# Attention and a feed-forward gate on one core: new load costs for the planner, a new list of moves, and tile 13 instead of tile 8 normalised by GpSimd

## The chip, the cores and the metric

The kernel runs on one core of a Trainium2 chip. The metric is the time of one execution on the device in microseconds (us). Before the change it is 640.19 us, the median of three runs (639.76, 640.19 and 640.46).

A core has five engines that run on their own and wait for one another through semaphores: TensorE (PE in the profile; its weight loads are PEld), VectorE (DVE), ScalarE (ACT), GpSimd (POOL) and SyncE (SP), which here only issues transfers. Each engine works through its own queue in order.

## The reference

All tensors are bfloat16. The input x has 2048 rows of 512. The kernel computes

```python
xn = _layernorm(x, axis=-1)
s = _A_ref(xn, A_wq, A_wk, A_wv, A_wo)
g = _silu(_B_ref(xn, B_w1, B_w2))
return x + s * g
```

`_A_ref` is attention with 32 heads of 16 elements each. All heads share one K and one V, made from xn by `wk` and `wv` (512x16). The scores are multiplied by 16 ** -0.5, go through a softmax over all 2048 keys, and are multiplied by V; the heads are joined and multiplied by `wo` (512x512). `_B_ref` is a feed-forward block: `silu(xn @ w1) @ w2` with a width of 1792.

## The kernel before

**Tiles and groups.** The rows of x are 16 tiles of 128; four tiles are a chunk of 512 rows. A group of attention is one chunk of queries with four heads; there are 32 groups, and each runs over 16 tiles of keys. A tile of scores has four blocks, one for each head, of 128 keys x 512 queries. The four heads stand in four row strips of TensorE, so blocks of different heads are multiplied at the same time.

**Two ways through the exponential.** Two blocks of a tile are a "run": TensorE writes them to one of two large PSUM banks (psA), ScalarE takes the exponential of both in one instruction (`exp_A`, L674) into pa_sb, and the bank is free again. In the other way (`exp_D`, L714) VectorE takes one block from a small PSUM bank (psD, psF, psO) and writes a 16-bit integer which, read as a bfloat16, is near the exponential; GpSimd then makes two shifted copies of the whole tile (`shift`, L739, an integer add), and the three copies, each with its own weight, are summed in the product with V. A tile on ScalarE needs one product with V for its four blocks, a tile on VectorE three. Such a product of four blocks is a "quad" (`emit_quad`, L769); all quads of a group add up in psO. When the group is complete, VectorE takes it out of psO, and normalises it (`gn1` to `gn4`, L882 to L908, with the product of numerators and reciprocals at L872).

**Dense work.** The projections q and w and the feed-forward products h and z are "jobs" of 4 or 14 column steps (L404). Each step takes as long as a quad, and both are called slots below. ScalarE makes a tanh for each h and z (L1116), VectorE takes every job out of its bank.

**The order is made when the kernel is built.** `Sched` holds a clock for each engine. `op` appends an instruction to its engine's queue, works out from what it reads and writes which semaphores it must wait for, and advances the clocks by a planned duration: the argument `cost` (for a transfer, `cost` is the time to its landing). The instructions are the same whatever `cost` is; only choices that look at the clocks depend on it.

The kernel is put together in four parts:

1. Fixed code: loads of x (`load_x`, L359) and of the weights (L368 to L374), statistics and normalisation of tiles 0 to 3 (`stats`, `aggr`, `normalise`, L464), the first transposes, K and Q, up to the first scores.
2. "Front", the loop at the end of the function: until the planner's clock of ScalarE passes `HANDOVER` (L297, 30.0) and all tiles are normalised (`settled`, L1351), each step is chosen by the clocks. The choices are tuned by the numbers of `RULES`; `PLAN` (L263) gives the letter of the rule for each stretch of 2 us (`STRETCH`) of that clock.
3. From there `follow` (L1448) takes the moves from a written list, `ORDER` (L298), letter by letter, without looking at the clocks.
4. `finish` (L1378) takes the end from `TAIL` (L299).

The letters of `ORDER`: R scores one run for ScalarE (two blocks), e takes its exponential, o opens a tile for VectorE, f scores one of its blocks into a bank, x lets VectorE take the oldest scored block, v is one quad, J opens a job, d and a digit do so many of its slots, t is a tanh, E lets VectorE take a finished job, 1 to 4 are the steps of a group's normalisation, H is a run of the last group, whose first four tiles of keys are cut by queries into three parts. In `TAIL`, q is a quad of such a part, n a step of its normalisation, P a piece of the last output projection, and r, C, M, G, A, X, Y, Z finish the last four tiles and store them.

**Normalising a tile of x.** For the tiles in `GPN` (L252) GpSimd does it, for the others VectorE. The set of tiles whose statistics are turned into reciprocal deviations together is a chunk, or for chunks 1 and 3 half a chunk (`SPLIT`). GpSimd takes the power and then, right behind it on its queue, normalises those of the set's tiles that are in `GPN`:

```python
            for t in ts:
                if t in GPN:
                    normalise(t, "gp")
```

Two normalised tiles are then transposed by TensorE (L476), copied by VectorE (L484), and give half a chunk of K (L507, copied at L519) and, with the other half, V (L533, L540). The copies of K for the odd groups go through four transfers per chunk (`move_K`, L525).

Of the kernel before, what the change touches and what calls it, by code (L numbers as in the profile page):

```python
# [5 lines left out]
ACT = mybir.ActivationFunctionType  # L6
# [7 lines left out]
P = 128  # L14
# [21 lines left out]
class Sched:  # L36
# [107 lines left out]
    def op(self, eng, fn, reads=(), writes=(), lane=None, cost=None):  # L144
        who = lane or eng
        if lane:
            self.lanes[lane] = eng
        n = self.done.get(who, 0)
        self.done[who] = n + 1
        deps = self.deps(eng, reads, writes)  # L150
        self.at[(who, n)] = self.model(eng, lane, cost, max([self.at[d] for d in deps.items()], default=0.0))
        clk = self.clock.setdefault(eng, {})
        waits = []
        cand = [(f, m) for f, m in deps.items() if clk.get(f, -1) < m]
        for f, m in cand:
            implied = False
            for f2, m2 in cand:
                if (f2, m2) != (f, m) and self.snap[(f2, m2)].get(f, -1) >= m:
                    implied = True
            if not implied:  # L160
                waits.append((f, m))
        for f, m in cand:
            for g, k in self.snap[(f, m)].items():
                if clk.get(g, -1) < k:
                    clk[g] = k
            if clk.get(f, -1) < m:
                clk[f] = m
        for f, m in waits:
            self.flagged.setdefault(f, set()).add(m)
        self.snap[(who, n)] = dict(clk)  # L170
        self.queues.setdefault(eng, []).append((fn, waits, who, n))
        for r in reads:
            self.readers.setdefault(r, {})[who] = n
        for w in writes:
            self.last_w[w] = (who, n)
            self.readers[w] = {}
        return who, n
# [36 lines left out]
def bass_recurrent_scan__grouped_kv_mqa__dense_activation_silu__prompt_kernel(  # L214
# [37 lines left out]
    GPN = (5, 8, 10)  # L252
# [10 lines left out]
    PLAN = "AAAAOAHAZHHYWcJEEEbbb"  # L263
# [16 lines left out]
        P=(0.25, 3.0, 0.65, 10, 1.2, 2.0, 0, 12, 0.2, 3, 3, 0.0, 0.35, 0.43, 0, 0.33, 0, 1),  # L280
# [10 lines left out]
        a=(0.3, 3.0, 0.65, 10, 1.2, 2.0, -4, 24, 0.2, 3, 3, 0.04, 9, 0.43, 0, 0.33, 0, 0),  # L291
        b=(0.2, 3.25, 0.65, 10, 1.2, 2.0, 0, 12, 0.2, 4, 3, 0.04, 9, 0.43, 0, 0.33, 0, 1),
# [6 lines left out]
    TAIL = "HvvvvHvvHvvq0Hq0q0q0q1q1q1q1n0PPn1n0PPn1q2q2n0q2n1n0Pq2n2n1Pr0r1C1n2G0PPPn2r2A0PPM1n2PG2r3X1Y1Z1G3A2A3"  # L299
    ALPHA = "".join(chr(x) for x in range(35, 127) if x != 92) + "".join(chr(x) for x in range(192, 255))  # L300

    with ExitStack() as es:
        def sb(name, shape, dt=BF16):
# [6 lines left out]
        wq_sb = sb("wq_sb", [P, NDC, D])  # L310
        wkn_sb = sb("wkn_sb", [P, NDC, DH])
# [37 lines left out]
        op = K.op  # L349
# [5 lines left out]
           reads=["ident"], writes=["ident"])  # L355
        xv = xf.rearrange("(t p) d -> p t d", p=P)
        ov = of.rearrange("(t p) d -> p t d", p=P)

        def load_x(a, b, queue="sp"):  # L359
            op(queue, lambda e: e.dma_start(x_sb[:, a:b, :], xv[:, a:b, :]), writes=[("x", t) for t in range(a, b)],  # L360
               lane=f"lx{a}", cost=(2.6 if queue == "sp" else 2.0) if b - a == 1 else {4: 4.6, 8: 5.0, 12: 5.6}[a])

        load_x(0, 1)
        load_x(1, 2, "a")
        load_x(2, 3)
        load_x(3, 4, "a")
        load_x(4, 8)
        op("sp", lambda e: e.dma_start(wkn_sb[:], A_wk.rearrange("(dc p) e -> p dc e", p=P)), writes=["wkn"], lane="lwk", cost=2.5)  # L368
        wqv = A_wq.rearrange("(dc p) n -> p dc n", p=P)
        op("sp", lambda e: e.dma_start(wq_sb[:, :, 0:P], wqv[:, :, 0:P]), writes=["wq0"], lane="lwq0", cost=4.0)  # L370
        op("sp", lambda e: e.dma_start(wv_sb[:], A_wv.rearrange("(dc p) e -> p dc e", p=P)), writes=["wv"], lane="lwv", cost=5.0)
        load_x(8, 12)
        load_x(12, 16)
        op("sp", lambda e: e.dma_start(wq_sb[:, :, P:D], wqv[:, :, P:D]), writes=["wq"], lane="lwq", cost=6.0)  # L374
        for j in range(NPH + 1):
            w = 1.0 if j == 0 else PH_W[j - 1]
            op("gp", lambda e, j=j, w=w: e.memset(vaug_sb[:, j, :, :].rearrange("p t (h e) -> p t h e", e=DH)[:, :, 0:3:2, :], w), writes=["vones"])
            op("gp", lambda e, j=j, w=w: e.memset(phw_sb[:, j:j + 1], w), writes=["phw"])
        op("gp", lambda e: e.memset(scr_i[:], 0), writes=["scri"])
        op("v", lambda e: e.memset(zero_sb[:], 0.0), writes=["zero"])  # L380
# [7 lines left out]
           reads=["wkn", "wkp"], writes=["wkp"])  # L388
# [55 lines left out]
        def rstd_pow(ts):  # L444
# [69 lines left out]
        def evac_K(c, bank, key, a, b, writes, eng="v"):  # L514
            dst, src, wr = kT_sb[0][:, c * NQ + a:c * NQ + b], bank[:, a:b], [("kT", 0, w) for w in writes]
            if eng == "a":
                op("a", lambda e: e.activation(dst, src, ACT.Copy), reads=[key], writes=wr)
            else:
                op("v", lambda e: e.tensor_copy(dst, src), reads=[key], writes=wr, cost=0.155 + (b - a) / 960)  # L519
# [52 lines left out]
        for t in tiles(0):  # L572
            normalise(t, "gp" if t in GPN else "v")
        first_T(0, psD[:, 0:NQ], "D", EV[0])
# [49 lines left out]
        gdone = [0.0] * (NGRP + 1)  # L624
        tok = {("q", 0, 0), ("kT", 0, 0), ("kT", 0, 1), ("kT", 1, 0)} | {(k, t) for k in ("nm", "T") for t in range(4)} | {("ag", t) for t in tiles(1)} | {("nm", t) for t in tiles(1) if t in GPN}
        hold = dict.fromkeys(BANKS + ("O",))
# [201 lines left out]
        def ln_ag(tk):  # L828
# [119 lines left out]
        for c in range(NC - 1):  # L948
            b = (c + 1) / NC
# [206 lines left out]
        dst = dict(open=[], idx=-1, fifo=[])  # L1156
# [352 lines left out]
        while not followed:  # L1509
            (SLIP, ROUND, KEEP, HOLD, AGES["gn1"], AGE, F_BEHIND, ENDQ, PVWAIT, LEAD, AHEAD, MARGIN, XGAIN, AIM, TWIN,  # L1510
             TGATE, FRESH, JOINT) = \
                RULES[PLAN[min(int(K.act_end / STRETCH), len(PLAN) - 1)]]
            if not followed and settled():
                if not w2_asked:
                    load_w2()
                    w2_asked = True
                follow(ORDER)
                followed = True
# [28 lines left out]
            if slots > 0:  # L1547
# [3 lines left out]
                if jb and slots >= 2:  # L1551
                    b = free_banks(t + 0.04)
# [68 lines left out]
```

## Time and profile before

| what | value |
|---|---|
| median of three runs | 640.19 us |
| lowest, highest run | 639.76, 640.46 us |
| profiled execution, its own time | 639.66 us |
| its span, first to last instruction | 637.8 us |
| TensorE busy | 631.1 us, 99% |
| ScalarE busy | 625.9 us, 98% |
| VectorE busy | 607.9 us, 95% |
| GpSimd busy | 434.8 us, 68% |
| granted TensorE clock | 0.999 |

The rows of groups read: line of the kernel, engine, operation, tile written and tiles read, shapes, count; behind the bar the busy time, the mean duration in ns, and the idle time of the engine just before these instructions with what ended it. A row of a timeline reads: start, length, engine, line, operation, tiles, shapes, count of the instructions merged, and in brackets the idle time before and what ended it. A row of the chain of waits reads start, length, what. A row of waits reads: who waited for whom, us in total, times, the longest. Instructions of one engine overlap a little, so lengths aren't pitches. The ends of matmuls are modelled, so a busy TensorE isn't one at its peak.

### The profile page before, as it was taken

Reading aid. Unit: us, or ns where it says so; the run is one execution under the profiler, and the core shown is the slowest. Engines: PE = TensorE matmul, PEld = TensorE weight load, DVE = VectorE, ACT = ScalarE, POOL = GpSimd, SP = SyncE. Lnnn points to the kernel's source line nnn. Section 1 sums busy time; section 2 is a strip of 40 time slices with the busy share of each in tenths; the row PEclk is TensorE's granted clock in tenths of the full one; section 3 lists DMA queues with packets and bytes.
Section 4 is the critical chain, followed back from the end, with each engine's and each line's share of the span. In section 5 each row is a group of like instructions: output and inputs, shape, how many; then the busy total and the mean of one; then the engine's idle time right before and its main releaser. Section 6 shows DMA issues by size and latency. Waiting matters only on the chain.

```text
span 637.8 us, 18784 instructions
## 1 busy us (share of the span) xinstructions
PE 631.1 (99%) x8225; PEld 197.1 (31%) x8227; DVE 607.9 (95%) x1049; ACT 625.9 (98%) x721; POOL 434.8 (68%) x438
## 2 busy tenths in 40 slices
PE   8999999999999999999999999999999999999997
PEld 3433332323233232332233323222323333233233
DVE  7989999999999999999999999999999999999994
ACT  8999999999999999999999999999999999999995
POOL 6556575667767777766766766688676676877662
PEclk9999999999999999999999999999999999999999
DMA  6380000000000000000000000001000000000003
GB/s 181 119 283 2 2 2 2 2 1 3 3 1 2 10 9 11 10 2 2 1 3 2 1 3 2 2 10 18 10 2 2 2 2 1 2 2 2 3 9 60
DMA packets 10082, 12.50 MB, mean 20 GB/s; under 512 B 2288, under 2 KB 9456, under 8 KB 9968
## 3 DMA queue, kind: packets, MB, share of 16 engines
q1 hardware_dynamic: 7840, 9.34, 4.5%
q0 software_dynamic: 1728, 1.57, 2.2%
q8 instruction: 64, 1.05, 0.7%
q10 hardware_dynamic: 432, 0.39, 0.2%
q14 instruction: 18, 0.15, 0.1%
HBM read 8.95 MB, written 4.19 MB: 21 GB/s over the span
## 4 chain that ended last, share of the span: by engine, by line
PE 94%; DVE 4%; ACT 1%; DMA 0%; issue 0%; DVEq 0%
PE psO L769 36%; PE psA L643 30%; PE psF L404 23%; PE psD L643 3%; DVE ph_sb L714 1%; DVE stats_sb L424 1%; DMA x_sb<-in_A_x_dram 0%; PE psA L692 0%; DVE xn_sb L465 0%; ACT xnT_sb L497 0%; DVE onb_sb L872 0%; PE psD L507 0%; PE psF L643 0%; ACT L459 0%; DVE xnT_sb L484 0%
## 5 line engine op out<-in xcount | busy, mean ns | idle before, releaser
L674 ACT ACTIVATE pa_sb<-psA 128x1024 bf16<-128x1024 f32 x630 | 593.2, 1067 | 3.1 <-PE psA L643 1.0
L739 POOL INT64_ADD ph_sb<-ph_sb x304 | 316.0, 1057 | 136.6 <-DVE ph_sb L714 136.2
L714 DVE TENSOR_SCALAR ph_sb<-psD 128x512 int16<-128x512 f32 x526 | 339.1, 679 | 13.0 <-PE psD L643 10.1
L769 PE MATMUL psO<-ph_sb,vaug_sb 128*32 128x512 bf16 x1824 | 224.3, 383 | 0.0
L769 PE MATMUL psO<-pa_sb,vaug_sb 128*32 128x512 bf16 (+1 forms) x1292 | 205.7, 378 | 0.0
L643 PE MATMUL psA<-qT_sb,kTa_sb 32*128 32x512 bf16 x640 | 123.9, 384 | 0.0
L739 POOL INT64_ADD x_sb<-x_sb x90 | 93.1, 1050 | 38.1 <-DVE x_sb L714 37.6
L643 PE MATMUL psA<-qT_sb,kTb_sb 32*128 32x512 bf16 x604 | 116.5, 384 | 0.0
L643 PE MATMUL psD<-qT_sb,kTa_sb 32*128 32x512 bf16 x336 | 110.1, 385 | 0.5 <-DVE ph_sb L714 0.5
L643 PE MATMUL psD<-qT_sb,kTb_sb 32*128 32x512 bf16 x347 | 110.6, 384 | 0.0
L714 DVE TENSOR_SCALAR x_sb<-psD 128x512 int16<-128x512 f32 x157 | 103.4, 680 | 3.8 <-PE psD L643 3.0
L769 PE MATMUL psO<-x_sb,vaug_sb 128*32 128x512 bf16 x540 | 93.2, 383 | 0.0
L769 PEld LDWEIGHTS psO<-ph_sb,vaug_sb 128*32 128x32 bf16 x1824 | 55.5, 95 | 53.0 <-issue 31.3
L643 PEld LDWEIGHTS psA<-qT_sb,kTa_sb 32*128 32x128 bf16 x640 | 30.1, 91 | 122.2 <-ACT pa_sb L674 95.8
L404 PE MATMUL psF<-w_sb,u_sb 128*32 128x512 bf16 x896 | 66.5, 384 | 0.0
L404 PE MATMUL psF<-xnT_sb,w_sb 128*32 128x512 bf16 x896 | 66.3, 384 | 0.0
L643 PEld LDWEIGHTS psA<-qT_sb,kTb_sb 32*128 32x128 bf16 x604 | 28.3, 91 | 119.0 <-ACT pa_sb L674 94.2
L769 PEld LDWEIGHTS psO<-pa_sb,vaug_sb 128*32 128x32 bf16 x1292 | 50.7, 95 | 37.2 <-issue 27.2
L714 DVE TENSOR_SCALAR ph_sb<-psF 128x512 int16<-128x512 f32 x70 | 47.5, 678 | 0.0
L1116 ACT ACTIVATE t_sb<-psF 128x512 bf16<-128x512 f32 x72 | 46.1, 640 | 0.0
L1135 DVE SCALAR_TENSOR_TENSOR u_sb<-t_sb,psF 128x512 bf16<-128x512 bf16 x56 | 37.8, 675 | 0.0
L643 PEld LDWEIGHTS psD<-qT_sb,kTb_sb 32*128 32x128 bf16 x347 | 29.0, 90 | 2.4 <-DVE ph_sb L714 0.2
(123 smaller groups left out, 387.6 us busy)
## 6 DMA issues: line engine op xcount, KB each, us to landing
w_sb<-in_B_w_dram SPq DMA_DIRECT2D x2, 1792.0 KB, 11.1
x_sb<-in_A_x_dram SPq DMA_DIRECT2D x3, 512.0 KB, 5.4
out_dram<-ob_sb POOLq DMA_DIRECT2D x12, 128.0 KB, 3.1
wop_sb<-in_A_wo_dram SPq DMA_DIRECT2D x1, 512.0 KB, 4.2
wq_sb<-in_A_wq_dram SPq DMA_DIRECT2D x1, 384.0 KB, 5.3
out_dram<-ob_sb SPq DMA_DIRECT2D x3, 128.0 KB, 1.7
x_sb<-in_A_x_dram SPq DMA_DIRECT2D x2, 128.0 KB, 2.8
x_sb<-in_A_x_dram ACTq DMA_DIRECT2D x2, 128.0 KB, 3.0
```

The source lines that it names most:

```text
L404: r = e.matmul(bank[32 * i:32 * i + 32, :], lhsT=w, rhs=rhs, start=start, stop=stop, tile_position=(0, 32 * i), skip_group_check=True)
L424: op("v", lambda e: e.bn_stats(stats_sb[:, t, :], x_sb[:, t, :]), reads=[("x", t)], writes=[("st", t)], cost=0.687)
L643: return e.matmul(ap, lhsT=kT_sb[g % 2][32 * i:32 * i + 32, kt * P:(kt + 1) * P], rhs=qT_sb[32 * i:32 * i + 32, c % 2, g // 2, :], start=T ...
L674: d = op("a", lambda e: e.activation(pa_sb[:, sl, :], psA[k][:, :], ACT.Exp, scale=ESCALE), reads=["A%d" % k], writes=[("pa", sl)], cost=2 ...
L714: d = op("v", lambda e: e.tensor_scalar(ph_ap(0, sl, 512 * pos, 512 * pos + m), src, float(PH_ONE + PH_BIAS), 0.0, op0=ALU.add, op1=ALU.ma ...
L739: d = op("gp", lambda e, j=j: e.int64_add(ph_ap(j, sl, 0, 4 * NQ).bitcast(I64), ph_ap(0, sl, 0, 4 * NQ).bitcast(I64), PH_SHIFT[j] * 0x0001 ...
L769: r = e.matmul(psO[32 * i:32 * i + 32, cs], lhsT=vaug_sb[:, p["v"], p["kt"], DH * (gi % 2):DH * (gi % 2) + 32], rhs=p["ap"], start=s0, sto ...
L1116: d = op("a", lambda e: e.activation(t_sb[:, n % 2, :], bank_ap(b), ACT.Tanh, scale=0.5 if jb[0] == "h" else 0.25), reads=[b], writes=[("t ...
L1135: op("v", lambda e: e.scalar_tensor_tensor(out=dst, in0=t_sb[:, n % 2, :], scalar=1.0, in1=src, op0=ALU.add, op1=ALU.mult), reads=tk["read ...
```

## The change

Four kinds of edits:

- `GPN` is (5, 10, 13) instead of (5, 8, 10): GpSimd normalises tile 13, VectorE tile 8.
- The planned costs of the loads: x tiles 4 to 7, 8 to 11 and 12 to 15 get 4.3, 5.5 and 6.0 instead of 4.6, 5.0 and 5.6; `wk` 4.9 instead of 2.5; the first part of `wq` 5.2 instead of 4.0. The copy of the first 128 columns of K on ScalarE gets the cost of its width. No instruction is added by these.
- `PLAN` has other letters for the stretches from 8 to 10 us (V for O) and from 28 us on (bbS for JEE).
- `ORDER` and `TAIL` are written anew. Both hold the same number of letters of nearly every kind (601 R, 605 e, 887 v, 784 x, 195 o, 99 J with 556 slots, 72 t, 4 H; f 782 before and 783 after), in another order.

```diff
-    GPN = (5, 8, 10)
+    GPN = (5, 10, 13)
...
-    PLAN = "AAAAOAHAZHHYWcJEEEbbb"
+    PLAN = "AAAAVAHAZHHYWcbbSEbbb"
...
-    ORDER = "xvxR1f01o02f14evxvR0exJ#2d1R1f05ed3xR0f13f02eE#vxR1eJ$2d2x
...
-xR0f02f13eR1exJÆ2d4xHeEÆvvHevvvHeJÇ2d4HeEÇ"
-    TAIL = "HvvvvHvvHvvq0Hq0q0q0q1q1q1q1n0PPn1n0PPn1q2q2n0q2n1n0Pq2n2n1Pr0r1C1n2G0PPPn2r2A0PPM1n2PG2r3X1Y1Z1G3A2A3"
+    ORDER = "xvR0eJ#2d1R1f11f00ed3xxR0o02f16evE#vR1f01exJ$2d2xR0f13ed2xvE
...
+xJÇ2d2xR0f13ed13vxR1f01ed1xvvHeEÇvvHevvHevvHe"
+    TAIL = "vvHvvHvvHvvHq0q0q0q0q1q1q1q1n0PPn1Pn0n1q2q2q2q2n0Pn1n0Pn1Pn2r0r1C1n2G0PPPn2r2A0Pn2PM1PG2r3X1Y1Z1G3A2A3"
...
         def load_x(a, b, queue="sp"):
-               lane=f"lx{a}", cost=(2.6 if queue == "sp" else 2.0) if b - a == 1 else {4: 4.6, 8: 5.0, 12: 5.6}[a])
+               lane=f"lx{a}", cost=(2.6 if queue == "sp" else 2.0) if b - a == 1 else {4: 4.3, 8: 5.5, 12: 6.0}[a])
...
-writes=["wkn"], lane="lwk", cost=2.5)
+writes=["wkn"], lane="lwk", cost=4.9)
...
-writes=["wq0"], lane="lwq0", cost=4.0)
+writes=["wq0"], lane="lwq0", cost=5.2)
...
         def evac_K(c, bank, key, a, b, writes, eng="v"):
             if eng == "a":
-                op("a", lambda e: e.activation(dst, src, ACT.Copy), reads=[key], writes=wr)
+                op("a", lambda e: e.activation(dst, src, ACT.Copy), reads=[key], writes=wr, cost=b - a)
```

More of the change, by code (lines that the diff above doesn't have):

```diff
@@ L367, in bass_recurrent_scan__grouped_kv_mqa__dense_activation_silu__prompt_kernel @@
         load_x(4, 8)
-        op("sp", lambda e: e.dma_start(wkn_sb[:], A_wk.rearrange("(dc p) e -> p dc e", p=P)), writes=["wkn"], lane="lwk", cost=2.5)
+        op("sp", lambda e: e.dma_start(wkn_sb[:], A_wk.rearrange("(dc p) e -> p dc e", p=P)), writes=["wkn"], lane="lwk", cost=4.9)
         wqv = A_wq.rearrange("(dc p) n -> p dc n", p=P)
-        op("sp", lambda e: e.dma_start(wq_sb[:, :, 0:P], wqv[:, :, 0:P]), writes=["wq0"], lane="lwq0", cost=4.0)
+        op("sp", lambda e: e.dma_start(wq_sb[:, :, 0:P], wqv[:, :, 0:P]), writes=["wq0"], lane="lwq0", cost=5.2)
         op("sp", lambda e: e.dma_start(wv_sb[:], A_wv.rearrange("(dc p) e -> p dc e", p=P)), writes=["wv"], lane="lwv", cost=5.0)
```

2 lines of the change are left out of this document (1 added, 1 removed).

## The prediction

> **What bounds the kernel now.** I read the page's first part for the engines, its chain of waits and its groups, then the timelines of ScalarE and TensorE, since two engines are nearly full.
>
> ```profile
> span 637.8 us, 18784 instructions
> PE 631.1 (99%) x8225; PEld 197.1 (31%) x8227; DVE 607.9 (95%) x1049; ACT 625.9 (98%) x721; POOL 434.8 (68%) x438
> PE 94%; DVE 4%; ACT 1%; DMA 0%; issue 0%; DVEq 0%
> L674 ACT ACTIVATE pa_sb<-psA 128x1024 bf16<-128x1024 f32 x630 | 593.2, 1067 | 3.1 <-PE psA L643 1.0 <-PE psD L643 1.0 <-PE psA L692 0.2
> L1116 ACT ACTIVATE t_sb<-psF 128x512 bf16<-128x512 f32 x72 | 46.1, 640 | 0.0
> PEld psA L643 <- ACT pa_sb L674: 190.0, 480, 0.5
> ```
>
> The chain says TensorE, but its busy time holds modelled ends, and the last row says that 480 times the score matmuls of TensorE waited for an exponential of ScalarE to give its bank back, 0.40 us each. The exponentials themselves sat idle for 3.1 us in all. So ScalarE sets the pace nearly everywhere, and TensorE's chain runs along it. Its timeline shows the pitch (start, length, what, count):
>
> ```profile
> 10.87 8.36 ACT L674 ACTIVATE pa_sb<-psA 128x1024 bf16<-128x1024 f32 x9 [0.59 <-PE psA L643]
> 11.79 19.09 ACT L674 ACTIVATE pa_sb<-psA 128x1024 bf16<-128x1024 f32 x20
> 31.74 10.18 ACT L674 ACTIVATE pa_sb<-psA 128x1024 bf16<-128x1024 f32 x11
> 41.70 0.71 ACT L1116 ACTIVATE t_sb<-psF 128x512 bf16<-128x512 f32 x1
> L674 ACT ACTIVATE pa_sb<-psA x630: 1017/1055/1293, 10.9 to 629.3; 128x1024 bf16<-128x1024 f32 x158
> ```
>
> An exponential alone lasts 1.02 us (the minimum of the last row), and they overlap: (8.36 - 1.02) / 8 and (10.18 - 1.02) / 10 both give 0.917 us from end to end. A tanh adds 41.70 + 0.71 - (31.74 + 10.18) = 0.49 us. The last rows of the same timeline:
>
> ```profile
> 606.53 5.66 ACT L674 ACTIVATE pa_sb<-psA 128x1024 bf16<-128x1024 f32 x6
> 612.54 1.02 ACT L674 ACTIVATE pa_sb<-psA 128x1024 bf16<-128x1024 f32 x1 [0.35 <-PE psD L643]
> 613.46 0.59 ACT L1116 ACTIVATE t_sb<-psF 128x512 bf16<-128x512 f32 x1
> 613.93 6.61 ACT L674 ACTIVATE pa_sb<-psA 128x1024 bf16<-128x1024 f32 x7
> 620.78 4.69 ACT L674 ACTIVATE pa_sb<-psA 128x1024 bf16<-128x1024 f32 x5 [0.23 <-PE psD L643]
> 625.67 4.69 ACT L674 ACTIVATE pa_sb<-psA 128x1024 bf16<-128x1024 f32 x5 [0.20 <-PE psA L692]
> ```
>
> The last exponential ends at 625.67 + 4.69 = 630.36. From 10.87 that is 619.49 us, and the work in it is 1.02 + 629 x 0.917 + 72 x 0.49 = 613.1 us. So ScalarE waits 6.4 us in all: 0.65 in Front (21 exponentials from 10.87 to 11.79 + 19.09 = 30.88 are 20.01 us against 1.02 + 20 x 0.917 = 19.36), and 5.75 in the listed part, of which 1.17 in the last 18 exponentials (612.19 to 630.36 is 18.17 against 18 x 0.917 + 0.49 = 17.0). The sum of the profiled execution is 10.87 before the first exponential, 613.1 of work, 6.4 of waits, 637.8 - 630.36 = 7.44 of end, and 639.66 - 637.8 = 1.86 around the span: 639.67. Its median stands 640.19 - 639.66 = 0.53 higher.
>
> **The work after the change.** Nothing in front of the first exponential changes: tiles 0 to 3 are normalised by VectorE in both kernels, and the first transposes, K and Q stand in the code and not in the planner's choice. So 10.87 stays. Read letter by letter, both lists hold 601 R, 605 e, 4 H, 72 t, 887 v, 784 x, 195 o, 99 jobs with 556 slots; both tails hold 4 H, 8 v, 12 q, 12 P. Where a group ends (letter 1) the number of its v is 16 + 2 x (its tiles on VectorE); that closes for 31 of 31 groups if Front makes 21 exponentials and opens two tiles on VectorE, as it does now. Then 630 exponentials and 72 tanh stay, and 613.1 us with them. The 7.44 us end keeps its order of r, C, G, A, X, Y, Z; only q, P and n change places before it: 0, with the last quads of TensorE as the bound either way. What can move is the 6.4 us of waits.
>
> **Load costs and PLAN.** These are numbers that the planner reckons with; no instruction has them. The loads themselves are issued in the same order on the same queues:
>
> ```profile
> wkn_sb<-in_A_wk_dram SPq DMA_DIRECT2D x1, 16.0 KB, 5.1
> 4.01 2.66 SPq L360 DMA_DIRECT2D x_sb<-in_A_x_dram  x2
> x_sb<-in_A_x_dram SPq DMA_DIRECT2D x3, 512.0 KB, 5.4
> 15.55 0.68 DVE L424 BATCH_NORM_STATS2 stats_sb<-x_sb 128x6 f32<-128x512 bf16 x1
> ```
>
> The last x load is issued by 4.01 + 2.66 = 6.67 and landed some 5.4 us later, before 12.1; tile 12 is first read at 15.55. So no landing holds anything after the first exponential, and truer landings can help only through the order that Front then picks. That order has one visible fault:
>
> ```profile
> 17.53 0.39 PE L643 MATMUL psA<-qT_sb,kTa_sb 32*128 32x512 bf16 x2
> 18.34 0.61 PE L507 MATMUL psD<-xnT_sb,wkp_sb 128*128 128x256 bf16 x4 [0.41 <-DVE xnT_sb L484]
> 18.88 0.39 PE L643 MATMUL psA<-qT_sb,kTa_sb 32*128 32x512 bf16 x2
> 6.19 1.38 DVE L465 TENSOR_SCALAR xn_sb<-x_sb,mv_sb,rstd_sb 128x512 bf16<-128x512 bf16 x4
> 11.02 0.41 DVE L465 TENSOR_SCALAR xn_sb<-x_sb,mv_sb,rstd_sb 128x512 bf16<-128x512 bf16 x1
> 16.57 1.11 DVE L465 TENSOR_SCALAR xn_sb<-x_sb,mv_sb,rstd_sb 128x512 bf16<-128x512 bf16 x2
> 17.60 0.68 DVE L484 COPY xnT_sb<-psD 128x1024 bf16<-128x1024 bf16 x1
> 10.28 2.11 POOL L465 TENSOR_SCALAR xn_sb<-x_sb,mv_sb,rstd_sb 128x512 bf16<-128x512 bf16 x1
> 16.64 4.28 POOL L465 TENSOR_SCALAR xn_sb<-x_sb,mv_sb,rstd_sb 128x512 bf16<-128x512 bf16 x2
> 20.89 0.22 POOL L447 TENSOR_SCALAR rstd_sb<-mv_sb 128x2 f32<-128x2 f32 x1
> ```
>
> At 18.34 TensorE stands 0.41 us in front of the second K of chunk 1, whose copy VectorE makes at 17.60, and a score whose keys are there waits behind it until 18.88. That starts the 0.65 us.
>
> **Tile 13 for tile 8.** GpSimd normalises 5, 8, 10 now (10.28, 16.64); it will do 5, 10, 13. VectorE gets tile 8 and gives up tile 13. Four normalisations in a row take 1.38 (6.19), so one more in a row is (1.38 - 0.41) / 3 = 0.32; the pair of 16.57 should take 0.73 and took 1.11, 0.38 more. Tile 8 costs 0.32 to 0.70, tile 13 gives back 0.32 to 0.41. GpSimd has tile 10 ready 2.14 us sooner, so tiles 10 and 11 can be transposed sooner; its power for tiles 12 and 13 no longer stands behind 16.64 + 4.28 = 20.92, and tile 13's 2.11 us then delays the power of 14 and 15, needed some 2 us later. Queued behind it are only tiles 14 and 15; exponential 25 is the first to need tile 12, at about 10.87 + 24 x 0.92 = 33, so this costs 0. Tile 8 can cost: if VectorE takes it ahead of the 17.60 copy, the wait of 0.41 grows by 0.32 to 0.70. So Front's term lies between -0.65 (its waits gone) and +0.70. I take -0.3, near the middle: the piece a choice can take is the 0.41, and VectorE stays as full.
>
> The Trainium skill (GPSIMD Engine Reference, 1. Specifications) says GpSimd's SBUF interfaces are shared with VectorE, with contention for VectorE instructions in a 2-port mode or with two SBUF inputs. By it each normalisation of VectorE beside GpSimd's would be held; the pair of 16.57 agrees (1.11), the one of 11.02 beside 10.28 doesn't (0.41), so by the rule Front would sit at its +0.70 end.
>
> **The list.** The pieces of TensorE's chain near the end price a gap between two exponentials:
>
> ```profile
> 610.80 0.32 PE psA L643 x2
> 611.20 0.98 PE psF L404 x16
> 612.50 0.76 PE psF L404 x12
> 610.01 0.55 PE psF L404 x8
> ```
>
> A score burst is 0.32, and 4, 3, 2 slots between are 0.98, 0.76, 0.55. Two gaps with 7 slots take 0.64 + 0.98 + 0.76 = 2.38 us against 2 x 0.917 = 1.83: 0.55 over; 6 slots 0.34 over, 5 slots 0.12, 8 slots 0.77. The three waits at 612.54, 620.78 and 625.67 stand behind pairs of 7, 6 and 7. Pairs without a tanh in the two lists, before to after: 5 slots 125 to 140, 6 slots 40 to 30, 7 slots 11 to 7, 8 slots 1 to 1. Excess before: 15.0 + 13.6 + 6.05 + 0.77 = 35.4; after: 16.8 + 10.2 + 3.85 + 0.77 = 31.6. Only 5.75 / 35.4 = 16% surfaces as waits, since TensorE has the 0.40 us of lead. I take the same share: -0.61. Bounds: -3.8 (all the excess removed had been waits) and +1.8 (15 more pairs of 5, none hidden, nothing removed).
>
> **Sum:** 639.67 - 0.30 - 0.61 = 638.76 for the profiled execution, 639.3 beside the median. 0.2% is 1.28 us (about what a measurement of this kernel can tell from no change): 638.91 and 641.47.
>
> **Rivals.**
> (1) The waits only move: the list's pairs were mostly hidden, and Front swaps one wait for another. For it: 84% of the excess is hidden now. Time 640.2.
> (2) Front and the end both run clean: -0.65, -1.17, and -0.49 (the same share of the other 4.58). For it: the new list ends with two v between its H where now three v, a job of four and H follow. Against it: VectorE stays 95% busy. 640.19 - 2.31 = 637.9.
> (3) Front opens a third tile on VectorE and makes 19 exponentials; the counts close for that too. -2 x 0.917 more: 637.4. Against it: that tile needs the last K chunk, which lands at the end of Front.
> (4) Slower: VectorE's normalisation of an attention group meets a GpSimd add.
>
> ```profile
> L872 DVE TENSOR_TENSOR onb_sb<-otr_sb,rcp_sb x19: 225/737/1600, 67.3 to 632.3; 128x512 bf16<-128x512 f32 x15, 128x64 bf16<-128x64 f32 x2, 128x256 bf16<-128x256 f32 x1, 128x128 bf16<-128x128 f32 x1
> 103.79 2.05 POOL L739 INT64_ADD ph_sb<-ph_sb  x2 [0.54 <-DVE ph_sb L714]
> 104.83 1.60 DVE L872 TENSOR_TENSOR onb_sb<-otr_sb,rcp_sb 128x512 bf16<-128x512 f32 x1
> 105.69 2.00 ACT L674 ACTIVATE pa_sb<-psA 128x1024 bf16<-128x1024 f32 x2
> 108.14 1.02 ACT L674 ACTIVATE pa_sb<-psA 128x1024 bf16<-128x1024 f32 x1 [0.45 <-PE psA L643]
> ```
>
> At 104.83 it took 1.60 against 0.74 while an add ran until 105.84, and an exponential ended 109.16 - 107.69 - 0.917 = 0.55 late, the largest wait of the list. It happens once in 15 now; a list made anew meets the adds at other places. From five of 15 on the gain is gone and more: 639.3 + 4 x 0.55 = 641.5. Against it: 14 of 15 went clear.
>
> The same rule of the Trainium skill (GPSIMD Engine Reference, 1. Specifications) names this pair, an instruction with two SBUF inputs beside GpSimd; the 1.60 us agrees with it.
>
> **How the numbers follow.** Forecast 0.45, its own range 638.7 to 640.3 (Front's -0.65 to +0.70, the list's share halved or doubled), of which 0.04 lies under 638.91; (1) 0.14; (2) 0.22; (3) 0.03; (4) 0.16. Faster 0.04 + 0.22 + 0.03 = 0.29, slower 0.16, the rest 0.55. The range 637.9 to 641.3 leaves out (3) and (4), 0.19.
>
> **What would show it.** The first exponential at about 10.9, 630 of them and 72 tanh: else the work was misread. Front: the 21st exponential ending under 30.88, and no wait of 0.4 of TensorE for a copy at 18. GpSimd's normalisations: three, the last near 20. List: the waits of ScalarE from 31 to 630 near 5.1 instead of 5.75, the rows of the last 18 exponentials without gaps. L872's maximum under 0.8 speaks against (4). Another end than 7.4 us, or waits of ScalarE above 6.4, would make the prediction wrong.

## The result and the profile after

| what | before | after |
|---|---|---|
| median (runs) | 639.76 us (6) | 637.67 us (6) |
| lowest, highest | 639.64, 640.46 | 637.54, 638.07 |
| ratio, 95% interval | | 0.9966 (0.9953 to 0.9979) |
| profiled execution, its span | 639.66, 637.8 us | 637.56, 635.8 us |
| ScalarE's waits: Front (21 exponentials) | 0.65 us | 0.07 us |
| list, up to the last 18 exponentials | 4.69 us | 4.45 us |
| last 18 exponentials | 1.18 us | 0.00 us |
| first exponential; end behind the last | 10.87; 7.43 us | 10.76; 7.52 us |

The kernel became 2.1 us faster; 639.3 was forecast, and 637.67 lies 0.23 under the range. A wait is here, and below, the time from the end of one exponential to the end of the next, less 0.9168 us (the 0.917 of the prediction; over 629 exponentials the rounding is 0.13 us) and less 0.49 for a tanh, added up over the trace. The differences are -0.58 in Front, -0.24 in the list, -1.18 at the end, -0.11 and +0.09 around them: -2.02. The spans, 637.79 and 635.76 us with one more digit, differ by 2.03.

From the page of the changed kernel, the rows that answer to those of before:

```profile
span 635.8 us, 18802 instructions
PE 628.9 (99%) x8225; PEld 195.9 (31%) x8227; DVE 605.6 (95%) x1049; ACT 625.3 (98%) x721; POOL 436.4 (69%) x438
PE 84%; ACT 9%; DVE 5%; issue 0%; DMA 0%; DVEq 0%
L674 ACT ACTIVATE pa_sb<-psA 128x1024 bf16<-128x1024 f32 x630 | 593.0, 1078 | 1.7 <-PE psA L643 0.6
```

The work is the same, 630 exponentials and as many matmuls. Their idle time fell from 3.1 to 1.7 us, and ScalarE now holds 9% of the chain, with 1% before. The timeline of ScalarE, its start and its last part:

```profile
10.76 27.77 ACT L674 ACTIVATE pa_sb<-psA 128x1024 bf16<-128x1024 f32 x30 [0.59 <-PE psA L643]
...
586.38 3.77 ACT L674 ACTIVATE pa_sb<-psA 128x1024 bf16<-128x1024 f32 x4 [0.25 <-PE psD L643]
...
597.22 3.95 ACT L674 ACTIVATE pa_sb<-psA 128x1024 bf16<-128x1024 f32 x4 [0.16 <-PE psD L643]
601.06 0.59 ACT L1116 ACTIVATE t_sb<-psF 128x512 bf16<-128x512 f32 x1
601.54 26.70 ACT L674 ACTIVATE pa_sb<-psA 128x1024 bf16<-128x1024 f32 x29
```

The last 29 exponentials take 26.70 us, and 1.02 + 28 x 0.917 is 26.70: no wait at all, where the kernel before has three that begin a row (612.54, 620.78, 625.67) and one of 0.08. The first 30 take 27.77 against 27.61. TensorE, VectorE and GpSimd in Front:

```profile
17.43 0.39 PE L643 MATMUL psA<-qT_sb,kTa_sb 32*128 32x512 bf16 x2
17.75 0.61 PE L507 MATMUL psD<-xnT_sb,wkp_sb 128*128 128x256 bf16 x4
18.29 0.39 PE L643 MATMUL psA<-qT_sb,kTa_sb 32*128 32x512 bf16 x2
```

```profile
16.46 0.41 DVE L465 TENSOR_SCALAR xn_sb<-x_sb,mv_sb,rstd_sb 128x512 bf16<-128x512 bf16 x1
16.79 0.68 DVE L484 COPY xnT_sb<-psD 128x1024 bf16<-128x1024 bf16 x1
17.39 0.73 DVE L465 TENSOR_SCALAR xn_sb<-x_sb,mv_sb,rstd_sb 128x512 bf16<-128x512 bf16 x2
...
16.54 2.22 POOL L465 TENSOR_SCALAR xn_sb<-x_sb,mv_sb,rstd_sb 128x512 bf16<-128x512 bf16 x1
...
20.42 2.09 POOL L465 TENSOR_SCALAR xn_sb<-x_sb,mv_sb,rstd_sb 128x512 bf16<-128x512 bf16 x1
```

VectorE makes the copy of the transposes at 16.79, between tile 8 and the pair of tiles 9 and 11, where the kernel before makes it behind that pair at 17.60; the second K starts at 17.75 without the 0.41 us that TensorE stood there. The group of L872:

```profile
L872 DVE TENSOR_TENSOR onb_sb<-otr_sb,rcp_sb x19: 224/732/743, 67.1 to 630.4; 128x512 bf16<-128x512 f32 x15, 128x64 bf16<-128x64 f32 x2, 128x256 bf16<-128x256 f32 x1, 128x128 bf16<-128x128 f32 x1
```

Its maximum is 0.74 us; the 1.60 of before is gone, and in the stretch from 105 to 115 us, where the kernel before waits 0.86 us, there is no wait.

### The profile page after: what moved, and what is told of

It reads as the page before. It is cut to its first block, busy times and chain, and to the rows that moved or that the text cites. A ratio compares the mean times of both kernels' runs of the same rounds, so it can differ in the third digit from the quotient of the medians.

```text
span 635.8 us, 18802 instructions
## 1 busy us (share of the span) xinstructions
PE 628.9 (99%) x8225; PEld 195.9 (31%) x8227; DVE 605.6 (95%) x1049; ACT 625.3 (98%) x721; POOL 436.4 (69%) x438
## 4 chain that ended last, share of the span: by engine, by line
PE 84%; ACT 9%; DVE 5%; issue 0%; DMA 0%; DVEq 0%
PE psO L769 32%; PE psA L643 27%; PE psF L404 20%; ACT pa_sb L674 8%; DVE ph_sb L714 3%; PE psD L643 2%; DVE x_sb L714 1%; ACT t_sb L1116 0%; PE psA L692 0%; DMA x_sb<-in_A_x_dram 0%; PE psD L507 0%; PE psD L476 0%; PE psF L643 0%; PE psD L533 0%; DVE stats_sb L424 0%
## 5 line engine op out<-in xcount | busy, mean ns | idle before, releaser
L769 PE MATMUL psO<-ph_sb,vaug_sb 128*32 128x512 bf16 x1824 | 227.7, 383 | 0.1
L769 PE MATMUL psO<-pa_sb,vaug_sb 128*32 128x512 bf16 (+1 forms) x1292 | 201.6, 378 | 0.2 <-DVE rcp_sb L923 0.2
L643 PE MATMUL psA<-qT_sb,kTa_sb 32*128 32x512 bf16 x632 | 122.1, 384 | 0.1
L643 PE MATMUL psA<-qT_sb,kTb_sb 32*128 32x512 bf16 x612 | 118.4, 385 | 0.3 <-ACT pa_sb L674 0.3
L643 PE MATMUL psD<-qT_sb,kTb_sb 32*128 32x512 bf16 x335 | 113.5, 384 | 0.0
L714 DVE TENSOR_SCALAR x_sb<-psD 128x512 int16<-128x512 f32 x153 | 100.7, 682 | 6.1 <-PE psD L643 5.3
L769 PE MATMUL psO<-x_sb,vaug_sb 128*32 128x512 bf16 x540 | 96.4, 383 | 0.0
L404 PE MATMUL psF<-xnT_sb,w_sb 128*32 128x512 bf16 x896 | 64.7, 383 | 0.0
L643 PEld LDWEIGHTS psD<-qT_sb,kTa_sb 32*128 32x128 bf16 x339 | 28.8, 91 | 2.2 <-DVE ph_sb L714 0.4
```

What stands on the lines that cost most here:

```text
L404: r = e.matmul(bank[32 * i:32 * i + 32, :], lhsT=w, rhs=rhs, start=start, stop=stop, tile_position=(0, 32 * i), skip_group_check=True)
L643: return e.matmul(ap, lhsT=kT_sb[g % 2][32 * i:32 * i + 32, kt * P:(kt + 1) * P], rhs=qT_sb[32 * i:32 * i + 32, c % 2, g // 2, :], start=T ...
L714: d = op("v", lambda e: e.tensor_scalar(ph_ap(0, sl, 512 * pos, 512 * pos + m), src, float(PH_ONE + PH_BIAS), 0.0, op0=ALU.add, op1=ALU.ma ...
L769: r = e.matmul(psO[32 * i:32 * i + 32, cs], lhsT=vaug_sb[:, p["v"], p["kt"], DH * (gi % 2):DH * (gi % 2) + 32], rhs=p["ap"], start=s0, sto ...
```

## The experiments

Times are medians, with the ratio to the kernel before of the same chip. In these traces each single wait of a stretch that was not edited comes back within 0.03 us from kernel to kernel (summed over the 590 exponentials of the list's middle within 0.11), so waits are read finer than the times. The expectations speak of TensorE's lead: how much later its score could have come without making ScalarE wait.

**Front: the copy alone (e1_copy_first).** In the kernel before, only the copy of tiles' transposes and the normalisation of tile 11 change places.

```diff
+                if pick is not None and pick["kind"] == "nm" and pick["t"] == 11:
+                    soon = [(x, tk) for x, tk in cand if tk["kind"] == "T" and x < first + 0.2]
+                    pick = min(soon, key=lambda p: p[0])[1] if soon else pick
```

> The kernel before with two neighbouring instructions of VectorE exchanged in Front: the copy of the second transpose of chunk 1 goes ahead of tile 11's normalisation. Nothing else differs. Theory A (each wait of ScalarE has a cause of its own and can be taken away alone): the second K of chunk 1 starts about 0.7 us sooner, TensorE's wait of 0.41 us goes, Front's waits fall from 0.65 to 0.1 and the span from 637.8 to 637.2. Rival B (TensorE is the bound, as the chain of waits says, so time saved early is waited for later): Front's waits fall, those behind it grow as much, span 637.8.

640.03 us, 1.0001 (0.9992 to 1.0010). Its timelines of ScalarE and VectorE:

```profile
11.69 24.25 ACT L674 ACTIVATE pa_sb<-psA 128x1024 bf16<-128x1024 f32 x26 [0.59 <-PE psA L643]
...
4.93 1.29 DVE L424 BATCH_NORM_STATS2 stats_sb<-x_sb 128x6 f32<-128x512 bf16 x2 [0.89 <-DMA x_sb<-in_A_x_dram]
```

Front's waits fell from 0.65 to 0.26, where theory A has 0.1; the others stayed, so rival B falls. The copy is worth 0.39 of the change's 0.58; the other 0.19 is left to the rest of Front's new order. The time did not show it. In the profiled execution (640.16) a load of x landed late (the second row) and all of the program began 0.8 us later. Of the eleven times five lie from 639.15 to 639.55 and six from 640.03 to 640.47; that the late load parts them is likely, but only one was profiled.

**The collision at 104.83 (e2_gn3_later).** Letter 3, the product at L872, goes behind three quads of the same stretch, out of the add's way.

```diff
-d3x3R0f03tevxvvE6R1f11o01f00evxR0e
+d3xR0f03tevxvvE63R1f11o01f00evxR0e
```

> The kernel before with one normalisation of an attention group (the one that took 1.60 us at 104.83) put two VectorE instructions later, where no GpSimd add should run. Theory A: it takes 0.74 us, the wait of 0.55 us at 108 goes, span 637.25. Rival B: the wait comes back within the next gaps, 637.8. Rival C: the normalisation meets another add there and takes 1.2 to 1.6 us again, 637.5 to 637.9.

639.21 us, 0.9997 (0.9988 to 1.0006). The waits of that stretch fell from 0.86 to 0.13 us, all others stayed. So the collision was worth 0.73 with what followed it, where the prediction had 0.55. The changed list has no such collision, and its removal is counted below with the same 0.73.

**The end made even, as the changed list has it (e3_even_end).** Two jobs are cut into parts between the runs. The new letters also hold one quad fewer (894 v in list and tail instead of 895), so this kernel, and with it e4 and e11 to e14, leaves out one product with V.

```diff
-JÅ2d1vxR1f11ed3xvEÅR0f02f13eR1exJÆ2d4xHeEÆvvHevvvHeJÇ2d4HeEÇ   TAIL HvvvvHvvHvvq0H
+JÅ2d2vxR1f11ed2xEÅR0f02f13evJÆ2d1R1exd3xHeEÆvvHevJÇ2d2Hed2HeEÇ   TAIL vvHvvvHvvHvvq0H
```

> The kernel before with the same moves spread evenly at its end: the gaps of the last exponentials hold 3, 2, 2, 3, 2, 3, 2, 2, 3 slots of TensorE where they held 2, 4, 0, 4, 2, 3, 4, 0, 4. Theory A: a gap's excess shows in full once TensorE's lead of 0.4 us is used up, and the end is where it is; three of the four waits there (0.34, 0.31 and the small one) go: -0.6, and no new one comes: span 637.2. The one of 0.46 at 612.5 lies in front of the edit and stays. Rival B (the prediction's share, 16% of the excess shows anywhere): -0.2, span 637.6.

640.52 us, 1.0013 (1.0004 to 1.0023): a little slower. The last 18 exponentials wait 1.42 us, 0.24 more than before; the larger part of the loss, 0.68, is an end of 8.11 us behind the last exponential instead of 7.43; why is open. TensorE in the last 18:

```profile
620.11 0.39 PE L643 MATMUL psA<-qT_sb,kTb_sb 32*128 32x512 bf16 x2
620.12 0.72 PE L643 MATMUL psD<-qT_sb,kTb_sb 32*128 32x512 bf16 x2
```

Two blocks for VectorE in one gap need 0.72 us instead of 0.39: the second stands for a bank that VectorE frees late. Even gaps alone do not clean the end.

**All three (e4_all_three).**

> The kernel before with the three edits of the other runs together (copy first, normalisation later, even end). Theory A: the gains add up, -0.55 - 0.55 - 0.6 = -1.7, span 636.1, within 0.4 of the changed kernel's 635.8 without its list, its load costs and its tile 13. Rival B: less than half of it, 637.0 or more.

639.01 us, 0.9992 (0.9983 to 1.0001). Waits 0.27, 0.13 and 1.41 us in the three places: the parts add up, and the end stays bad. Theory A's -1.7 did not come: the span is 637.9, of which 0.75 us is a later start.

**The end made uneven in the changed kernel (e5_heavy_end).**

```diff
-xJÇ2d2xR0f13ed13vxR1f01ed1xvvHeEÇvvHevvHevvHe     TAIL vvHvvHvvHvvHq0
+xvxR0f13e3vxR1f01exvvHevvHevvvHeJÇ2d4HeEÇ         TAIL HvvvvHvvHvvHq0
```

> The changed kernel with its last job of four slots moved back between the last runs, as the kernel before has it: the slots of the last seven gaps between scores are then 2, 3, 4, 0, 4, 2, 2 as before, but the last 19 gaps together still hold 40 slots (before: 51). Theory S (the sum decides: TensorE needs about 0.63 us for a score burst with one slot and 0.21 for each further slot, so 51 slots in 19 gaps are 18.2 us against 17.0 of ScalarE and 40 slots 16.3): the waits of ScalarE in the last 18 exponentials stay at 0 to 0.15 us, and the time within 0.3 us of the changed kernel. Theory P (the pair of gaps just ahead of a wait decides, as the prediction priced it): the wait that the kernel before has there, 0.31 us behind the gaps 3 and 4, comes back, 0.3 to 0.55 us.

638.01 us, 0.9976 (0.9966 to 0.9986); its span is 636.1 us, 0.3 above the changed kernel's. Its last 29 exponentials:

```profile
601.57 26.91 ACT L674 ACTIVATE pa_sb<-psA 128x1024 bf16<-128x1024 f32 x29
```

One wait of 0.22 us came back, behind the job of four slots. Neither theory has it right. The gaps one by one have: just ahead TensorE's lead is 0.33 us, a gap of three slots takes 1.085 - 0.917 = 0.17 of it and one of four 1.30 - 0.917 = 0.38, which leaves 0.22 short.

**Pairs made even, slots kept (e6_even_pairs); two slots left out (e7_fewer_slots).**

```diff
-R0exvvR0f03o02f16ed2xvxR1f01ed4x1R1f10
-JÅ2d1vxR1f11ed3xvEÅR0f02f13eR1exJÆ2d4xHe
+R0exvvd1R0f03o02f16ed2xvxR1f01ed3x1R1f10
+JÅ2d2vxR1f11ed2xvEÅR0f02eJÆ2d1f13R1exd3xHe
```

> The kernel before with the gaps ahead of its two longest end waits made even (2, 3, 4, 4 becomes 3, 3, 3, 4; 2, 4, 0, 4 becomes 3, 3, 1, 3), only by moving slots of a job one gap forward or back; the last 19 gaps still hold 51 slots, all else is as before. Theory P: the waits of 0.46 at 612.5 and 0.34 at 620.8 go, the last 18 exponentials wait 0.3 to 0.5 us instead of 1.18. Theory S: they wait 0.9 to 1.2, since TensorE has as much to do as before.

```diff
-                for m in items:
+                for m in (items[-1:] if jb == ("w", 8) else items):
```

> The kernel before with two slots left out of the projection of one tile of rows (two of the four products that are summed for it are missing), in the gaps at 615.4 and 618.6 us, where ScalarE does not wait; the gaps ahead of the waits at 620.8 and 625.7 keep their slots. Theory S: two slots are 0.42 us of TensorE, so the two waits behind (0.34 and 0.31) lose 0.35 to 0.45 together, and TensorE's last matmul comes 0.3 to 0.45 earlier. Theory P: the two waits stay within 0.1 us, and only the end may move. In both the wait of 0.46 at 612.5 stays.

e6: 640.40 us, 1.0011 (1.0003 to 1.0020); the last 18 wait 1.74 us, far over what theory P has and over theory S's 1.2, and just ahead of them stands a new wait of 0.17. (One of the moved slots goes to the gap ahead of the last 19, so these hold 50.) e7: 639.67 us, 1.0001 (0.9992 to 1.0010); 1.09 us. The end of e6 and then of e7:

```profile
622.16 4.07 ACT L674 ACTIVATE pa_sb<-psA 128x1024 bf16<-128x1024 f32 x4 [0.24 <-PE psA L643]
626.51 4.69 ACT L674 ACTIVATE pa_sb<-psA 128x1024 bf16<-128x1024 f32 x5 [0.28 <-PE psA L692]
```

```profile
620.80 4.69 ACT L674 ACTIVATE pa_sb<-psA 128x1024 bf16<-128x1024 f32 x5 [0.22 <-PE psD L643]
625.69 4.69 ACT L674 ACTIVATE pa_sb<-psA 128x1024 bf16<-128x1024 f32 x5 [0.20 <-PE psA L692]
```

In e7 the two waits stand where they were (0.33 and 0.31), although TensorE has 0.43 us less to do just ahead, and its last matmul comes no earlier. Theory S falls as it was put: time that TensorE gains is not carried over to the next jobs. What stops it first is ScalarE: the scores at 616.05 and 616.99 start 0.06 and 0.08 us after the exponential two before them has ended and so freed their bank, and 0.06 is the least in the trace of the kernel before too. In e6 theory P falls: four of its waits are 0.17 us, each behind a gap of three slots with no lead left (1.085 - 0.917), and making the gaps even put such gaps in a row.

**Single slots moved everywhere in the changed list (e8_smooth).** For example:

```diff
-1d3xR1f01f30ed2xR0f13exd2xR1f01o01f30ed4xxR0f12
+1d4xR1f01f30ed3xR0f13exd2xR1f01o01f30ed2xxR0f12
```

> The changed kernel with some 25 single slots of jobs moved one gap forward or back, where gaps of 4 slots stand beside gaps of 1 or 2; no other letter of the list moves. The waits of ScalarE between the 22nd exponential and the last 18 are 4.45 us in the changed kernel. If they are TensorE's backlog over a few neighbouring gaps (theory S), adding up the gaps with the measured pitches gives about 1.4 us less: 2.7 to 3.5 us of waits there, 636.3 us in all. If most of them come from banks that VectorE frees late, they stay at 4.0 to 4.7, and the time at 637.7.

639.75 us, 1.0006 (0.9997 to 1.0014); its span is 637.8 us, 2.1 above the changed kernel's. The waits between Front and the last 18 exponentials are 6.41 us instead of 4.45; 2.7 to 3.5 were expected. TensorE at the place of the example, in e8 and then in the changed kernel:

```profile
408.56 0.39 PE L643 MATMUL psA<-qT_sb,kTa_sb 32*128 32x512 bf16 x2
408.57 0.72 PE L643 MATMUL psD<-qT_sb,kTa_sb 32*128 32x512 bf16 x2
```

```profile
407.89 0.39 PE L643 MATMUL psA<-qT_sb,kTa_sb 32*128 32x512 bf16 x2
407.89 0.39 PE L643 MATMUL psD<-qT_sb,kTa_sb 32*128 32x512 bf16 x2
```

With two slots instead of four ahead of the two blocks for VectorE, their bank is not free, and TensorE stands 0.33 us (0.72 against 0.39). A large gap is also the time in which VectorE catches up. In all, seven blocks for VectorE start 0.18 to 0.34 us behind their scores in e8 that do not in the changed kernel, and about half of the 1.96 us follows within four gaps of them. The cause of the other half is open.

**Front alone and list alone (e9_front_alone, e10_list_alone).** The two lists meet in the same state at the 76th exponential, where both open job J2, so their parts can be exchanged there; GPN, load costs and PLAN go with the first part.

```
e9:  ORDER = changed list up to J22, then the list before from there on, and the tail before
e10: ORDER = list before up to J22, then the changed list from there on, and the changed tail
```

> The changed kernel's GPN, load costs, PLAN and its list as far as the 76th exponential (at 72 us), then the list and the tail of the kernel before. If Front's gain and the list's are independent, ScalarE waits 0.07 us in Front and 5.8 to 6.0 after it, as the kernel before does: 0.5 to 0.6 us less in the profiled work, about 639.1 us. If the late waits of the list depend on what Front leaves, they differ by more than 0.2 us from the kernel before.

> The complement: GPN, load costs, PLAN and the list as far as the 76th exponential from the kernel before, then the changed list and tail. Independent parts: 0.65 us of waits in Front and 4.4 to 4.5 after it as in the changed kernel, none in the last 18: 1.4 us less than before, about 638.2 us. If tile 13 on GpSimd and Front's order carried the gain, it stays within 0.5 us of the kernel before.

e9: 639.05 us (639.1 expected), 0.9993 (0.9984 to 1.0002), 0.59 below the kernel before of its chip, though the interval takes in no change; waits 0.06 in Front and 5.86 behind it. e10: 638.50 us, 0.9984 (0.9975 to 0.9993); waits 0.65 in Front, none in the last 18, but 5.23 between instead of 4.45. Nearly all of that surplus is one wait. VectorE, GpSimd and ScalarE in e10:

```profile
572.59 1.64 DVE L872 TENSOR_TENSOR onb_sb<-otr_sb,rcp_sb 128x512 bf16<-128x512 f32 x1
...
571.58 2.05 POOL L739 INT64_ADD ph_sb<-ph_sb  x2
...
576.76 1.02 ACT L674 ACTIVATE pa_sb<-psA 128x1024 bf16<-128x1024 f32 x1 [0.76 <-PE psD L643]
```

and the same place in the changed kernel:

```profile
571.99 0.73 DVE L872 TENSOR_TENSOR onb_sb<-otr_sb,rcp_sb 128x512 bf16<-128x512 f32 x1
...
570.98 2.60 POOL L739 INT64_ADD ph_sb<-ph_sb  x2
```

The same two instructions meet in both. In one VectorE waits (1.64, the adds 2.05), in the other GpSimd does (adds 2.60, VectorE 0.73). The eleven times of e10 fall in two heaps, seven of 638.12 to 638.55 and four of 639.51 to 640.00; the lower heap is the 638.2 that independent parts give. The one that was profiled (639.53) is of the upper heap; besides the wait its end is 7.90 us, 0.38 longer than the changed kernel's with the same tail, and why is open. By the waits Front and list act independently but for this tie; that the lower heap is the tie won by VectorE is likely, but no execution of it was profiled.

**What holds the end (e11_one_f to e14_later_and_fewer).** e11 takes the two blocks of e3 apart, e12 also leaves slots out, e13 opens job JÆ a gap later than e11, e14 does both.

```diff
-EÅR0f02f13evJÆ2d1R1exd3xHe     e3
+EÅR0f02evJÆ2d1R1f13exd3xHe     e11, e12
+EÅR0f02evR1f13exJÆ2d4xHe       e13, e14
...
-                for m in items:
+                for m in (items[-1:] if k == "w" and jb[1] in (9, 10, 11) else items):     e12, e14
```

> The even end of e3_even_end with its two blocks for VectorE in one gap (f02 f13) put into two gaps; slots as there. Theory V (TensorE stood there for a bank that VectorE had not freed): the 0.24 us that TensorE stood at 620.1 and the wait of 0.31 at 621.8 go, the last 18 exponentials wait 1.0 to 1.15 us instead of 1.42. Theory S (TensorE has too many slots, so the waits only move): 1.3 to 1.45 in all, later.

> The same, with six slots left out of the last three projections (half of the products that are summed for three tiles of rows are missing): 44 slots in the last 19 gaps and no gap over 3. If a clean end needs both, even gaps and fewer slots than ScalarE's pace allows, the waits behind 613 us fall to 0.1 to 0.25 and the last 18 exponentials wait 0.55 to 0.7, all but 0.15 of it at 612.5; TensorE's last matmul comes 0.8 to 1.2 us earlier than in e3_even_end. If VectorE sets the end, 0.5 us or more of waits remain behind 613 us.

> The even end of e11_one_f with job JÆ opened one gap later, so that a whole score lies between VectorE's copy of the job bank (0.68 us, for which TensorE stood 0.22 us at 621.1 in e11) and the next job's first slot. 50 slots in the last 19 gaps. Theory B (the one bank for jobs held TensorE in the even ends): TensorE no longer stands for that copy (under 0.05 us), and what is left is the count of slots: by the pitches of the gaps (0.65, 0.87, 1.085, 1.30 us for 1 to 4 slots against 0.917) 0.9 to 1.1 us of waits in the last 18 exponentials instead of 1.62. If the bank was not the cause: 1.4 us or more.

> The same with seven slots left out of the last three projections (products that are summed for three tiles of rows are missing): 43 slots in the last 19 gaps, against 40 in the changed kernel and 51 before. Theory B with the count of slots: the waits of 0.46 at 612.5 and 0.085 at 618.6 stay, nothing over 0.1 follows: 0.55 to 0.65 in all, and TensorE's last matmul comes 0.9 to 1.3 us earlier than before (633.99). If something else of VectorE holds the end, 0.2 us or more follow behind 619.

The waits of all variants of the end, by the count of slots in the last 19 gaps between scores:

| kernel | slots | largest gap of the last 14 | waits of the last 18 | of them without the one at 612.5 us |
|---|---|---|---|---|
| before | 51 | 4 | 1.18 | 0.72 |
| e3 | 50 | 3 | 1.42 | 0.96 |
| e6 | 50 | 4 | 1.74 | 1.45 |
| e7 | 49 | 4 | 1.09 | 0.63 |
| e11 | 50 | 3 | 1.62 | 1.16 |
| e12 | 44 | 3 | 0.80 | 0.35 |
| e13 | 50 | 4 | 1.21 | 0.75 |
| e14 | 43 | 3 | 0.54 | 0.09 |
| e5 | 40 | 4 | 0.22 | 0.22 |
| after | 40 | 3 | 0.00 | 0.00 |

Times: e11 640.35 us, 1.0011 (1.0002 to 1.0020); e12 639.42, 0.9997 (0.9988 to 1.0006); e13 640.16, 1.0008 (0.9999 to 1.0018); e14 639.41, 0.9998 (0.9988 to 1.0007). In e11 theory V falls: the blocks are apart and the waits are larger. What TensorE stands for, in e11 and then in e12:

```profile
621.12 0.40 PE L404 MATMUL psF<-wop_sb,xn_sb 128*32 128x512 bf16 x4 [0.22 <-DVE ob_sb L1147]
...
620.38 0.68 DVE L1147 SCALAR_TENSOR_TENSOR ob_sb<-psF,tmp_sb 128x512 bf16<-128x512 f32 x1
```

```profile
620.90 0.40 PE L404 MATMUL psF<-wop_sb,xn_sb 128*32 128x512 bf16 x4 [0.43 <-DVE ob_sb L1148]
```

The next job's first slot waits until VectorE has taken the job before out of the bank that both use (0.68 us, begun when its queue comes to it). With six slots fewer TensorE arrives earlier and stands longer, 0.43 instead of 0.22, and 0.35 us of waits are left behind 613 us, where 0.1 to 0.25 were expected. e13 and e14 put a score between. In e13 the job's slot no longer stands, but the block for VectorE beside that score does, 0.22 us, until the same copy ends:

```profile
621.15 0.39 PE L643 MATMUL psA<-qT_sb,kTb_sb 32*128 32x512 bf16 x2
621.38 0.37 PE L643 MATMUL psD<-qT_sb,kTb_sb 32*128 32x512 bf16 x1
...
622.66 0.39 PE L692 MATMUL psA<-qT_sb,kTb_sb 32*128 32x256 bf16 x4
```

From score to score are 1.51 us with four slots, 0.21 over the 1.30 of other gaps of four. So theory B's first half fails, and 1.21 less this 0.21 is the 0.9 to 1.1 that it has for 50 slots. In e14:

```profile
613.75 15.78 ACT L674 ACTIVATE pa_sb<-psA 128x1024 bf16<-128x1024 f32 x17
```

Here 1.02 + 16 x 0.917 is 15.69: 0.09, and nothing follows 619 us. TensorE stands 0.2 us for that copy here too, but at a score that begins 0.06 us after its bank is free, so the lead covers it. So a clean end took both: few enough slots, and VectorE's copy where TensorE is ahead. How much each is worth is not parted cleanly, since e14 has one slot fewer than e12. The gain does not reach the time: e14's end behind the last exponential is 7.95 us (637.48 less 629.53) instead of 7.43, and TensorE's last matmul came only 0.56 us earlier, counted from the first exponential, with 0.9 to 1.3 expected. Why this tail is longer is open.

## Why the prediction was wrong

- **The work and the two ends held.** First exponential 10.76 (10.87), 630 exponentials, 72 tanh, 0.917 and 0.49 us, an end of 7.52 (7.43): only the waits moved, from 6.52 to 4.52. What happened is rival (2), "Front and the end both run clean", 637.9; it had 0.22. That its 637.9 is so near is partly luck: its -2.31 is more than the measured -2.03, and the median that it starts from, 640.19 of three runs, is 639.76 of six. Of the forecast's miss of 1.6 us these 0.43 are the base; the rest is a gain of 0.91 forecast and 2.03 measured in the spans.
- **Load costs and PLAN:** no load is waited for behind the first exponential, as argued. Their only way in is the order that Front picks, and no run parts them there from tile 13.
- **Front's order: the wait that goes was named right, the size was too small.** GpSimd normalises three tiles, the last at 20.42, as said. Forecast -0.30, measured -0.58, inside -0.65 to +0.70. "The piece a choice can take is the 0.41" was right (e1: 0.39); that the other waits behind it go with the rest of the order (0.19) was put in the bound only. Whether tile 13, the load costs or PLAN put the copy forward is open. Tile 8 was not in the way: it stands ahead of the copy, which still came 0.81 us earlier, and the pair at 17.39 took 0.73 us beside GpSimd, not 1.11.
- **The price of the list is the step that failed, and under it the reading of TensorE's lead.** "I take the same share: -0.61" priced the list from one share, 16%, of an excess counted by pairs. Measured is -1.42 in three pieces that no common share gives: the end -1.18, where the whole went; the collision -0.73 (e2), which was in the waits but not in the count; and the rest of the middle, 3.96 to 4.45, which grew by 0.49. The prices of the gaps were good (0.87, 1.085 and 1.30 us from score to score for 2, 3 and 4 slots, over the scores that did not wait for ScalarE); the lead was not. "TensorE has the 0.40 us of lead" rests on the row of 480 waits, and this row was misread. It is of PEld, the weight loads, which are soon done and then idle while the matmuls go on. From the kernel before:

```profile
617.86 0.38 PE L769 MATMUL psO<-x_sb,vaug_sb 128*32 128x512 bf16 x2
617.87 0.38 PE L769 MATMUL psO<-pa_sb,vaug_sb 128*32 128x512 bf16 x1
617.87 0.38 PE L769 MATMUL psO<-x_sb,vaug_sb 128*32 128x512 bf16 x1
618.18 0.09 PEld L643 LDWEIGHTS psA<-qT_sb,kTb_sb 32*128 32x128 bf16 x2 [0.42 <-ACT pa_sb L674]
618.18 0.39 PE L643 MATMUL psA<-qT_sb,kTb_sb 32*128 32x512 bf16 x2
```

The load of 618.18 has idled for 0.42 us, but its score follows the matmuls before it without a gap. Between 30 and 600 us the waits of PE itself are one row:

```profile
PE psD L643 <- DVE ph_sb L714: 0.5, 1, 0.5
```

The starts of the instructions, which are not modelled, say the same: over 620 scores of that trace a score starts 0.29 us (median) after the exponential two before it has freed its bank, 0.06 at the least, and under 0.1 in only 39. So it is not so that "ScalarE sets the pace nearly everywhere": TensorE seldom stands for ScalarE, and the two are about equally full. The lead follows from the end of an exponential less the start of its score: 1.45 us when the exponential waits for it (1.02 and the 0.43 from score to exponential, the least of the 622), and 0.15 us more at the median. That is the lead, 0.15 us and not 0.40. A gap of two slots gives 0.05 of it back, one of three takes 0.17, one of four 0.38. With 51 slots in 19 gaps it cannot recover, with 40 it can, and e5 shows the same account at a single wait.

- **The rest of the middle** is not settled. e10 shows that it goes with the list and not with Front; e8 shows that evening out the slots does not cure it, and in part why: VectorE's banks are then late. An estimate from the prices above (0.23 us for a gap of none and 0.65 for one of one slot beside them, a lead of 0.33 at most as ahead of e5's wait), added up gap by gap, gives 2.5 us of waits in the middle before and 2.7 after, for 3.96 without the collision and 4.45 measured. So it has the sign, and some 60% of the size. At the end it gives 1.7 and 0.0, for 1.18 and 0.00 measured. For the middle of e8 it gives 2.4, for 6.41 measured.
- **Rival (1)**, that the waits only move, came true in kind in e3, e6, e8 and e11, where waits came up at other places, not in the change. **Rival (3)** did not come: 21 exponentials in Front. **Rival (4)** did not come either, but its ground was misread: "14 of 15 went clear" is not so, as the last section shows. On the rule of the Trainium skill (GPSIMD Engine Reference, 1. Specifications), by which Front would sit at +0.70: the pair at 17.39 ran at 0.73 us while GpSimd normalised (16.54 for 2.22), so the trace shows no holding there. Whether these instructions run in the 2-port mode that the rule names, no row shows. Of the 1.11 of before, which the prediction took as agreeing, only the second instruction is long (0.78 us at 16.90); in e1, where the copy stands between the two, it takes 0.41 beside the same instruction of GpSimd. Why it is long is open.

## What to carry to other kernels

Where two engines are both nearly full, don't price a reordering by the average share of an excess that surfaces. Go through the stretch gap by gap with the lead that is left, because a lead of 0.15 us is spent by the first large gap. That account alone missed e8 by far: before evening out a schedule, look for what the uneven gap was giving time to, here a bank that a third engine had yet to free. Read the idle time of weight loads as what it is, not as TensorE standing. Read the gain of one part from the waits of its stretch, since the start of the program varies by more than the part is worth.

## What the runs showed of the hardware

**Who comes first runs at full speed.** In the kernel before, nine of the fifteen full products at L872 overlap an add of GpSimd. In seven VectorE began first or within 5 ns of the add: it took 0.72 to 0.74 us, and the add 1.40 to 1.61 instead of 1.04. In two the add was first: at 104.83, by 0.03 us, VectorE took 1.60; at 595.81, when 0.22 us of the add were left, 0.80. One of the seven, VectorE then GpSimd:

```profile
232.38 0.72 DVE L872 TENSOR_TENSOR onb_sb<-otr_sb,rcp_sb 128x512 bf16<-128x512 f32 x1
...
232.56 2.43 POOL L739 INT64_ADD ph_sb<-ph_sb  x2 [0.33 <-DVE ph_sb L714]
```

Two adds are 2.05 us elsewhere and 2.43 here. So these two seem to run one after the other for the most part, and only the second pays: in all nine it is longer by what the first had left, less 0.15 to 0.19 us. In the changed kernel the two at 572 us begin within 0.01 us of each other, and in e10 too, with the other winner: a few ns decide over some 0.9 us.

**The start varies.** In the profiles of these kernels, whose code ahead of the first exponential is the same, it starts between 10.69 and 12.54 us. In e1 statistics stood 0.89 us for a load of x, in the kernel before the same three ran back to back; in e9 (12.54) that load explains about 1 us of the 1.7, the rest is open.
